# The opening's dummy products of a fused RWKV-6 and squared-ReLU kernel: 46 bf16 products become 12 fp32 products

## The chip, the cores and the metric

The kernel runs on one core of one Trainium2 chip. The metric is the device time of one execution in microseconds, the median of several runs. A profile is one execution recorded by the hardware profiler.

## The reference

Two stages. The first is a linear attention with a decaying state (4 batches, 8 heads, 768 positions, head size 48); the second is a two-layer network without gating on its output (3072 tokens, 384 to 2048 to 384), all in float32 at the interface.

```
for t in range(S):
    cur = einsum('bhd,bhe->bhde', u[None] * kt, vt)
    y[:, :, t] = einsum('bhd,bhde->bhe', rt, state + cur)
    state = wt[:, :, :, None] * state + einsum('bhd,bhe->bhde', kt, vt)
x = y, as (3072, 384)
h = x @ w_in;  g = max(h, 0)**2;  out = g @ w_out
```

## The kernel before

The 3072 tokens are cut into 12 steps of 256 positions (three for each batch), and a step into two chunks of 128. For each step the attention runs in the chunked form: logarithms of the decays (`ww_`, `lw_`), their running sums by products with triangular matrices (`cum_`, lines 324 to 328), exponentials (`exp_`, `ac_`), scaled copies of r and k (`rd_`), their transposes (`tr_` on TensorE with the copies `rkt_`, line 374, in the first steps; by DMA later), the score blocks (`p_`, line 420, masked in `pm_`), the state update (`su_`, `ts_`, `sn_`), the outputs (`y_`, `yc_`, `ysb_`) and their transposes for the second stage (`yt_`, `xt_`). The second stage is `m1_` (x times w_in, line 536, 48 products of 256 columns for a step in eight groups), a relu and a square (`rl_`, `sq_`, lines 545 to 555) and `m2_` (times w_out, line 561, 32 products of 384 columns), scaled out by `os_` and stored. All products of the two stages have bf16 operands.

The order of the work is written out by hand. `ORDER` is one string of words; the kernel goes through it word by word, and each engine issues its instructions in that order, with no reordering across words. A word is an operation with its arguments; what stands behind `=` is the engine (A ScalarE, V VectorE, G GpSimd), what stands behind `:` the PSUM banks. The loads (`ld.s.w`, `.k`, `.r`, `.v` of step s; `ld.g.i` and `ld.g.o` for the quarters of w_in and w_out) all go through SyncE's queue. w_in and w_out arrive as fp32 in four staging buffers and are cast to bf16 by the words `cast.i.g` and `cast.o.g` (line 200).

The change touches the word `warm_.n.i`: n products of the tile `warm`, which holds zeros, with itself, into a PSUM bank that is free at that point; nothing reads their result. `i` chooses the bank. There are eight such words, all among the first steps' work: with n = 11 and 8 ahead of and behind the first `cum_`, 3 and 5 around the transposes of step 0, 3 and 2 in step 0's output, 4 in step 1 and 10 ahead of the transposes of step 2. `warm` itself is cleared by the first instruction of `constants()` on VectorE (line 227), ahead of the other constants and of the zeros in `rdec_buf` and `kdec_buf`.

Of the kernel before, what the change touches and what calls it, by code (L numbers as in the profile page):

```python
# [8 lines left out]
FP32 = mybir.dt.float32  # L9
FP16 = mybir.dt.float16  # L10
BF16 = mybir.dt.bfloat16
# [3 lines left out]


ORDER = """
ld.0.w ld.0.k ld.0.r ld.0.u ld.1.w ww_.0=V lw_.0 warm_.11.5 cum_.0:0 kw_.0=G exp_.0 rd_.0.1 ld.0.v warm_.8.5
tr_.0.1:0 rkt_.0.1=A ld.1.k ld.1.r rw_.0=G ld.2.w ku_.0=G rd_.0.0 ld.1.v warm_.3.5 tr_.0.0:1 ww_.1=V
rkt_.0.0=A qp_.0=V ld.2.r v_.0=A warm_.5.5 p_.0.0:m p_.0.1:1 ac_.0 lw_.1 q_.0 su_.0:b ld.2.k cum_.1:0  # L20
ts_.0.0=A kw_.1=G pm_.0.0 pm_.0.1 vs_.0.0=A sn_.0.0 ld.1.i exp_.1 rw_.1=G vs_.0.1=A qs_.0=A rd_.1.1 ku_.1=G
warm_.3.2 yc_.0.1:1 ld.0.i ac_.1 ts_.0.1=V rd_.1.0 warm_.2.2 tr_.1.1:0 sn_.0.1 y_.0:1 rkt_.1.1=A vq_.0=V
tr_.1.0:1 ww_.2=G ld.2.i v_.1=A rkt_.1.0=V ysb_.0=V vs_.1.1=A warm_.4.2 p_.1.1:0 qp_.1=G su_.1:m ld.2.v
pm_.1.1 lw_.2 yt_.0:0 cum_.2:1 ld.3.i ts_.1.0=V rw_.2=G q_.1 exp_.2 kw_.2=G xt_.0=V vs_.1.0=A rd_.2.0 qs_.1=G
ac_.2 cast.i.1=A rd_.2.1 warm_.10.1 tr_.2.0:1 sn_.1.0 p_.1.0:0 ku_.2=G ts_.1.1=V yc_.1.1:1 tr_.2.1:0
cast.i.0=A pm_.1.0 ld.0.o m1_.0.3:0 ld.3.w rkt_.2.1=V m1_.0.2:1 vq_.1=G rkt_.2.0=V y_.1:1 rl_.0.3=A yc_.1.0:1
rl_.0.2=V p_.2.0:0 m1_.0.1:0 ld.1.o ysb_.1=V cast.i.2=G m1_.0.0:1 rl_.0.1=A pm_.2.0 yt_.1:0 ld.3.r rl_.0.0=A
m1_.0.5:0 v_.2=A xt_.1=V qp_.2=G sn_.1.1 m1_.0.4:1 rl_.0.5=A p_.2.1:1 su_.2:b sq_.0.0=A rl_.0.4=V ld.2.o
# [68 lines left out]
def kernel(  # L97
# [17 lines left out]
    C = 128  # L115
# [21 lines left out]
    consts = ctx.enter_context(tc.tile_pool(name="consts", bufs=1))  # L137
# [71 lines left out]

    warm = consts.tile([C, 512], BF16)
    tri_strict = consts.tile([C, C], BF16)
    tri_incl_neg = consts.tile([C, C], BF16)
    ident = consts.tile([C, C], BF16)
# [367 lines left out]
    def ld(n, x, h=None):  # L583
# [3 lines left out]
        ld=ld, cast=cast, ww_=ww_, lw_=lw_, v_=v_, vs_=vs_, rw_=rw_, kw_=kw_, ku_=ku_, qp_=qp_, q_=q_, qs_=qs_,  # L587
        vq_=vq_, cum_=cum_, al_=al_, exp_=exp_, ac_=ac_, rd_=rd_, tr_=tr_, rkt_=rkt_, dtr_=dtr_, p_=p_, pm_=pm_,
        su_=su_, ts_=ts_, sn_=sn_, y_=y_, yc_=yc_, ysb_=ysb_, yt_=yt_, xt_=xt_, dyt_=dyt_,
# [42 lines left out]
```

## Time and profile before

| | |
|---|---|
| time, median of 3 runs | 182.44 us (182.27 to 183.0) |
| span of the profiled execution, first to last instruction | 182.2 us |
| instructions | 5695 |
| TensorE busy | 171.8 us, 94% |
| VectorE, ScalarE, GpSimd busy | 130.0, 132.7, 122.7 us |
| dummy products (line 578) | 46, the first at 1.2 us, the last at 24.0 us |
| DMA, mean over the span | 197 GB/s |

The profile has no time of the execution beside its span; the median of the runs lies 0.24 us above the span. Times in the views count from the first instruction. PE is TensorE's products, PEld its weight loads, DVE VectorE, ACT ScalarE, POOL GpSimd, SPq SyncE's queue of loads and stores. A product's length is its latency; products overlap, so what one adds to the stream is read from the distance of two starts.

### The profile page before, as it was taken

The page shows a single profiled execution, that of the slowest core. Times are in us where ns is not written, and L with a number is a line of the kernel's source. Part 1 is how long each engine was busy: PE and PEld are TensorE (multiplying, and loading weights), DVE is VectorE, ACT ScalarE, POOL GpSimd, SP SyncE. Part 2 cuts the span into 40 slices and gives each one's busy share as a digit, 9 for nine tenths or more (in the row PEclk, how much of TensorE's full clock was granted, in tenths as well). Part 3 has the DMA queues.
Part 4 walks back from the last instruction along what each step waited for, and adds up shares of the span by engine and source line. Part 5 has one row for each costly group of instructions (what it writes and reads, how often), then busy time and mean ns, then how long its engine had stood idle before and what let it go on. Part 6 is the DMA issues. An engine that isn't in the chain of part 4 may idle for free.

```text
span 182.2 us, 5695 instructions
## 1 busy us (share of the span) xinstructions
PE 171.8 (94%) x2385; PEld 123.4 (68%) x2385; DVE 130.0 (71%) x195; ACT 132.7 (73%) x235; POOL 122.7 (67%) x140
## 2 busy tenths in 40 slices
PE   7986787999999999999899999999999999999992
PEld 2453556788686777777677777786877767777761
DVE  5488998787795998796677989885779675355120
ACT  4289665999779998869987997667979268552631
POOL 6539994999768999997949999699599413000000
PEclk9999999999999999999999999999999999999998
DMA  5999899999999989899999999997859520250023
GB/s 138 263 263 240 221 359 350 337 314 311 234 274 230 261 158 270 99 247 130 239 296 205 193 270 172 252 189 193 171 109 195 150 47 0 86 144 33 0 86 130
DMA packets 79208, 35.81 MB, mean 197 GB/s; under 512 B 72400, under 2 KB 77648, under 8 KB 79184
## 3 DMA queue, kind: packets, MB, share of 16 engines
q1 hardware_dynamic: 79184, 35.46, 85.9%
q8 instruction: 18, 0.29, 0.7%
q14 instruction: 6, 0.05, 0.1%
HBM read 25.36 MB, written 4.72 MB: 165 GB/s over the span
## 4 chain that ended last, share of the span: by engine, by line
PE 75%; SPq 10%; DMA 8%; ACT 4%; issue 1%; DVE 1%; ACTq 0%
PE bk L561 32%; PE m L536 32%; SPq L178 8%; DMA w_st<-in_moe_w_in_dram 5%; PE att L420 3%; DMA rT<-rdec_buf 2%; PE att L483 2%; PE att L493 2%; PE att L446 1%; ACT gt L545 1%; PE att L326 1%; ACT wi_sb L200 1%; PE bk L516 1%; SPq L188 1%; SPq L205 1%
## 5 line engine op out<-in xcount | busy, mean ns | idle before, releaser
L536 PE MATMUL m<-xT,wi_sb 128*128 128x256 bf16 x576 | 74.0, 273 | 1.3 <-ACT gt L545 1.2
L561 PE MATMUL bk<-wo_sb,gt 128*128 128x384 bf16 x384 | 71.9, 326 | 0.0
L536 PEld LDWEIGHTS <-wi_sb 128*128 128x128 bf16 x576 | 54.8, 98 | 13.0 <-issue 0.9
L561 PEld LDWEIGHTS <-gt 128*128 128x128 bf16 x384 | 36.9, 98 | 19.2
L545 ACT ACTIVATE gt<-m 128x512 f16<-128x512 f32 x56 | 33.0, 595 | 22.3 <-PE m L536 21.9
L553 ACT ACTIVATE gt<-gt 128x1024 bf16<-128x1024 f16 x42 | 43.3, 1051 | 1.4 <-DVE gt L547 1.1
L547 DVE TENSOR_SCALAR gt<-m 128x512 f16<-128x512 f32 x40 | 27.0, 686 | 9.6 <-PE m L536 9.3
L434 DVE TENSOR_TENSOR pmT<-att,mask 128x1024 bf16<-128x1024 f32 x20 | 23.9, 1218 | 4.5 <-PE att L420 4.5
L297 POOL TENSOR_TENSOR ku<-k_raw,u_bc 128x768 f32<-128x768 f32 x12 | 21.8, 1819 | 0.2 <-DMA u_bc<-in_u_dram 0.2
L302 POOL TENSOR_TENSOR ku<-ku,r_raw 128x768 f32<-128x768 f32 x11 | 20.7, 1881 | 0.2
L316 POOL TENSOR_TENSOR ku<-v_sh,qs 128x768 f32<-128x768 bf16 x11 | 16.3, 1479 | 4.9 <-ACT qs L277 4.8
L277 ACT CAST v_sh<-v_raw 64x384 bf16<-64x384 f32 x34 | 17.3, 508 | 0.4
L290 POOL TENSOR_TENSOR k_raw<-k_raw,w_raw 128x384 f32<-128x384 f32 x12 | 12.2, 1013 | 6.4 <-DMA k_raw<-in_k_dram 6.3
L286 POOL TENSOR_TENSOR r_raw<-r_raw,w_raw 128x384 f32<-128x384 f32 x12 | 12.0, 1000 | 6.4 <-DMA r_raw<-in_r_dram 6.4
L504 DVE TENSOR_TENSOR y_sb<-att,ku 128x768 bf16<-128x768 f32 x12 | 11.4, 953 | 5.5 <-issue 1.6
L461 POOL TENSOR_TENSOR S<-t_state,ac_buf 128x192 bf16<-128x192 f32 x20 | 10.2, 512 | 6.4 <-DVE t_state L456 3.4
L361 DVE TENSOR_TENSOR kdec_buf<-k_raw,att 128x768 bf16<-128x768 f32 x12 | 11.4, 949 | 3.4 <-ACT att L340 2.8
L358 DVE TENSOR_TENSOR rdec_buf<-r_raw,att 128x384 bf16<-128x384 f32 x24 | 12.1, 547 | 2.2 <-ACT att L340 1.1
L340 ACT ACTIVATE att<-att 128x768 f32<-128x768 f32 x12 | 9.6, 798 | 3.1 <-PE att L328 1.9
L568 ACT ACTIVATE o_sb<-bk 128x384 f32<-128x384 f32 x13 | 6.3, 485 | 7.4 <-PE bk L561 7.3
L307 DVE TENSOR_REDUCE q<-ku 128x16 f32<-128x768 f32 x12 | 11.3, 943 | 0.0
L578 PE MATMUL att<-warm 128*128 128x512 bf16 x27 | 9.1, 492 | 1.2 <-DVE half_ones L228 1.2
(80 smaller groups left out, 188.8 us busy)
## 6 DMA issues: line engine op xcount, KB each, us to landing
w_raw<-in_w_dram SPq DMA_DIRECT2D x12, 384.0 KB, 5.3
k_raw<-in_k_dram SPq DMA_DIRECT2D x12, 384.0 KB, 5.9
r_raw<-in_r_dram SPq DMA_DIRECT2D x12, 384.0 KB, 5.7
v_raw<-in_v_dram SPq DMA_DIRECT2D x12, 384.0 KB, 5.8
out_dram<-o_sb SPq DMA_DIRECT2D x24, 192.0 KB, 2.5
w_st<-in_moe_w_in_dram SPq DMA_DIRECT2D x4, 768.0 KB, 11.1
w_st<-in_moe_w_out_dram SPq DMA_DIRECT2D x4, 768.0 KB, 9.3
rT<-rdec_buf SPq DMA_TRANSPOSE x16, 4.1
```

Source lines behind the costliest of these rows:

```text
L178: nc.sync.dma_start(out=t[:, hs, at:at + 2, :].rearrange("p h j d -> p h (j d)"), in_=src[b, hs, i * T:(i + 1) * T, :].rearrange("h (p j) ...
L277: copy(out[j * Q:(j + 1) * Q, c], src[c * Q:(c + 1) * Q, :, j])
L290: tensor_mul("kw_", s, h)(raw["k", s][:, hs, 0, :], raw["k", s][:, hs, 1, :], raw["w", s][:, hs, 1, :])
L297: tensor_mul("ku_", s, h)(tiles["ku", s][:, hs], raw["k", s][:, hs, 1:3, :], u_bc[:, hs, None, :].to_broadcast([C, n, 2, D]))
L302: tensor_mul("qp_", s, h)(ku, ku, raw["r", s][:, heads(h), 0:2, :])
L316: tensor_mul("vq_", s)(vq[:], tiles["vs", s][:], tiles["qs", s][:, :, :, None].to_broadcast([C, 2, H, D]))
L434: nc.vector.tensor_mul(pmT, ps_p[:].rearrange("p e (x t) -> p (e x) t", t=C), mk.to_broadcast([C, 8, C]))
L536: nc.tensor.matmul(ps1[:, j, :], wi_sb[:, n // 4, kk, n % 4 * 128:(n % 4 + 1) * 128], tiles["xT", s][:, :, kk, :], start=(kk == 0), stop=( ...
L545: nc.scalar.activation(rl, m1, AF.Relu, scale=RS)
L547: nc.vector.tensor_scalar(out=rl, in0=m1, scalar1=RS, scalar2=0.0, op0=ALU.mult, op1=ALU.max)
L553: nc.scalar.activation(gt, rl, AF.Square)
L561: nc.tensor.matmul(m2, gt[:, n, c * C:(c + 1) * C], wo_sb[:, n, :], start=(n == 0), stop=(n == NT - 1))
```

## The change

The tile `warm` becomes fp32, and the eight counts are divided by about four: 11, 8, 3, 5, 3, 2, 4, 10 become 3, 2, 1, 1, 1, 1, 1, 2. The words keep their places in the order and their banks. The rest of the order and of the kernel is the same.

```diff
 ORDER = """
-ld.0.w ld.0.k ld.0.r ld.0.u ld.1.w ww_.0=V lw_.0 warm_.11.5 cum_.0:0 kw_.0=G exp_.0 rd_.0.1 ld.0.v warm_.8.5
-tr_.0.1:0 rkt_.0.1=A ld.1.k ld.1.r rw_.0=G ld.2.w ku_.0=G rd_.0.0 ld.1.v warm_.3.5 tr_.0.0:1 ww_.1=V
-rkt_.0.0=A qp_.0=V ld.2.r v_.0=A warm_.5.5 p_.0.0:m p_.0.1:1 ac_.0 lw_.1 q_.0 su_.0:b ld.2.k cum_.1:0
+ld.0.w ld.0.k ld.0.r ld.0.u ld.1.w ww_.0=V lw_.0 warm_.3.5 cum_.0:0 kw_.0=G exp_.0 rd_.0.1 ld.0.v warm_.2.5
+tr_.0.1:0 rkt_.0.1=A ld.1.k ld.1.r rw_.0=G ld.2.w ku_.0=G rd_.0.0 ld.1.v warm_.1.5 tr_.0.0:1 ww_.1=V
+rkt_.0.0=A qp_.0=V ld.2.r v_.0=A warm_.1.5 p_.0.0:m p_.0.1:1 ac_.0 lw_.1 q_.0 su_.0:b ld.2.k cum_.1:0
...
-warm_.3.2 yc_.0.1:1 ld.0.i ac_.1 ts_.0.1=V rd_.1.0 warm_.2.2 tr_.1.1:0 sn_.0.1 y_.0:1 rkt_.1.1=A vq_.0=V
-tr_.1.0:1 ww_.2=G ld.2.i v_.1=A rkt_.1.0=V ysb_.0=V vs_.1.1=A warm_.4.2 p_.1.1:0 qp_.1=G su_.1:m ld.2.v
+warm_.1.2 yc_.0.1:1 ld.0.i ac_.1 ts_.0.1=V rd_.1.0 warm_.1.2 tr_.1.1:0 sn_.0.1 y_.0:1 rkt_.1.1=A vq_.0=V
+tr_.1.0:1 ww_.2=G ld.2.i v_.1=A rkt_.1.0=V ysb_.0=V vs_.1.1=A warm_.1.2 p_.1.1:0 qp_.1=G su_.1:m ld.2.v
...
-ac_.2 cast.i.1=A rd_.2.1 warm_.10.1 tr_.2.0:1 sn_.1.0 p_.1.0:0 ku_.2=G ts_.1.1=V yc_.1.1:1 tr_.2.1:0
+ac_.2 cast.i.1=A rd_.2.1 warm_.2.1 tr_.2.0:1 sn_.1.0 p_.1.0:0 ku_.2=G ts_.1.1=V yc_.1.1:1 tr_.2.1:0
...
-    warm = consts.tile([C, 512], BF16)
+    warm = consts.tile([C, 512], FP32)
```

## The prediction

> **What bounds the kernel now.** I read the page first: the span, the busy engines, the clock and the chain that ended last.
>
> ```profile
> span 182.2 us, 5695 instructions
> ...
> PE 171.8 (94%) x2385; PEld 123.4 (68%) x2385; DVE 130.0 (71%) x195; ACT 132.7 (73%) x235; POOL 122.7 (67%) x140
> ...
> PEclk9999999999999999999999999999999999999998
> ...
> PE 75%; SPq 10%; DMA 8%; ACT 4%; issue 1%; DVE 1%; ACTq 0%
> ```
>
> TensorE carries three quarters of the chain. The other 18% of DMA and its queue need a place, because the change touches only the opening. So the second view was the chain in order of time, for its first 48 us. From 1.87 us on it is nothing but the load queue, and it ends like this:
>
> ```profile
> 17.59 1.33 SPq L188
> ...
> 18.96 9.57 DMA w_st<-in_moe_w_in_dram
> ...
> 28.55 1.47 ACT wi_sb L200
> 30.02 0.51 ACT gt L545
> ...
> 30.57 1.47 PE m L536 x12
> ```
>
> The load of a quarter of w_in lands at 18.96 + 9.57 = 28.53, ScalarE casts it, a relu queued behind that cast frees a bank of m1, and at 30.57 TensorE gets its next first-layer product. Nothing that TensorE did earlier is on this chain. After 30.57 the chain is TensorE nearly all the way. So the opening's products matter in three ways only: if they come so late that they are still running at 30.57, if they make the loads late, or if they change the clock at which the rest runs.
>
> The third view is TensorE's own row of time for the opening. The columns are start, length, engine, line, operation, tiles, count, and the idle time before it with what ended that.
>
> ```profile
> 1.19 4.87 PE L578 MATMUL att<-warm 128*128 128x512 bf16 x11 [1.19 <-DVE half_ones L228]
> 5.85 0.29 PE L324 MATMUL att<-half_ones,lw_buf 128*128 128x2 bf16 x4
> ...
> 6.60 2.14 PE L578 MATMUL att<-warm 128*128 128x512 bf16 x8
> 8.74 0.62 PE L374 MATMUL bk<-ident,kdec_buf 128*128 128x128 bf16 x8
> 9.20 0.81 PE L578 MATMUL att<-warm 128*128 128x512 bf16 x3
> 9.84 0.61 PE L374 MATMUL bk<-ident,rdec_buf 128*128 128x128 bf16 x8
> ...
> 15.25 0.31 PE L493 MATMUL att<-S,rT 64*64 64x48 bf16 x16 [0.88 <-DVE pmT L434]
> 15.50 0.61 PE L578 MATMUL m<-warm 128*128 128x512 bf16 x2
> 16.16 0.62 PE L374 MATMUL bk<-ident,kdec_buf 128*128 128x128 bf16 x8
> ...
> 17.81 0.23 PE L374 MATMUL bk<-ident,rdec_buf 128*128 128x128 bf16 x1 [0.62 <-DVE rdec_buf L358]
> ...
> 22.11 2.32 PE L578 MATMUL bk<-warm 128*128 128x512 bf16 x10
> 24.51 0.23 PE L374 MATMUL bk<-ident,rdec_buf 128*128 128x128 bf16 x1
> ...
> 28.94 0.40 PE L420 MATMUL att<-rT,kT 64*64 64x128 bf16 x16
> 30.57 1.47 PE L536 MATMUL m<-xT,wi_sb 128*128 128x256 bf16 x12 [1.23 <-ACT gt L545]
> ```
>
> TensorE stands idle for 1.23 us ahead of 30.57. That is the cover under which an opening that is late disappears.
>
> **What a dummy costs, and the clock.** The same line L578 in three stretches (1 to 5.5 us, 6.5 to 7.5, 9 to 11.4), and its weight loads over the span; the columns are count, then shortest, median and longest in ns.
>
> ```profile
> L578 PE MATMUL att<-warm x11: 607/634/634, 1.2 to 5.4; 128*128 128x512 bf16 x11
> ...
> L578 PE MATMUL att<-warm x4: 379/398/627, 6.6 to 7.5; 128*128 128x512 bf16 x4
> ...
> L578 PE MATMUL att<-warm x8: 379/379/379, 9.2 to 11.2; 128*128 128x512 bf16 x8
> ...
> L578 PEld LDWEIGHTS <-warm x46: 96/98/151, 1.2 to 23.8; 128*128 128x128 bf16 x46
> ```
>
> The page's clock line reads 9 from its first slice on, but one and the same product takes 634 ns until 5.4 us and 379 ns from 9.2 us, with the change between 6.6 and 7.5. So TensorE starts slow and comes up about 6 us after its first dummy. The starts give what one product adds to the stream: (5.85 − 1.19) / 11 = 0.424 us slow, (9.84 − 9.20) / 3 = 0.213 us fast. The weight load (98 ns) fits under the product before it.
>
> **The change, part by part.**
>
> *Counts.* 46 dummies become 12, in the same eight places: 11, 8, 3, 5, 3, 2, 4, 10 become 3, 2, 1, 1, 1, 1, 1, 2. As built, each fp32 product is one instruction, without the separate weight load that each bf16 one had. DVE, ScalarE, GpSimd and the load queue keep their order.
>
> *Price of an fp32 product.* The trace has none. The lower bound is a bf16 product of that shape, 0.424 slow or 0.213 fast. For the upper one, I split each wide number into two narrow halves: four partial products, each with a weight load that nothing hides, 4 × (0.424 + 0.098) = 2.09 slow and 4 × (0.213 + 0.098) = 1.24 fast. I take four hidden passes, 1.70 slow and 0.85 fast, because in this kernel's stream of 512 columns the weight load of every dummy is hidden. The Trainium skill, "FP8 and Floating Point Precision", TensorE Precision Notes, also gives four passes for true fp32; no run here shows it yet. Passes by place are then 12, 8, 4, 4, 4, 4, 4, 8 against 11, 8, 3, 5, 3, 2, 4, 10: 48 against 46.
>
> *The clearing of the dummy tile* doubles in bytes. The VectorE and ScalarE rows that this and the next steps need:
>
> ```profile
> 0.86 0.27 DVE L227 MEMSET warm<- 128x256 uint32 x1 [0.86 <-PEq L616]
> ...
> 1.55 0.48 DVE L232 MEMSET rdec_buf<- 128x512 uint32 x1 [0.17 <-issue]
> ...
> 4.57 0.56 DVE L264 TENSOR_TENSOR ww<-w_raw 128x384 f32<-128x384 f32 x1 [0.91 <-DMA w_raw<-in_w_dram]
> 7.73 0.95 DVE L361 TENSOR_TENSOR kdec_buf<-k_raw,att 128x768 bf16<-128x768 f32 x1 [2.60 <-ACT att L340]
> 8.60 1.01 DVE L358 TENSOR_TENSOR rdec_buf<-r_raw,att 128x384 bf16<-128x384 f32 x2
> 10.25 0.77 DVE L264 TENSOR_TENSOR ww<-w_raw 128x384 f32<-128x384 f32 x1 [0.63 <-DMA w_raw<-in_w_dram]
> ...
> 32.41 0.56 DVE L521 COPY xT<-bk 128x768 bf16<-128x768 bf16 x1 [0.99 <-PE bk L516]
> ```
>
> ```profile
> 5.22 0.52 ACT L268 ACTIVATE lw_buf<-ww 128x384 bf16<-128x384 f32 x1 [2.17 <-DVE ww L264]
> ...
> 25.24 1.47 ACT L200 CAST wi_sb<-w_st 128x1536 bf16<-128x1536 f32 x1
> 28.55 1.47 ACT L200 CAST wi_sb<-w_st 128x1536 bf16<-128x1536 f32 x1 [1.84 <-DMA w_st<-in_moe_w_in_dram]
> ```
>
> The clearing of 128x512 words took 0.48 in rdec_buf's row, so warm's goes from 0.27 to 0.48, +0.21. VectorE's later clearings move by 0.21 under the 0.91 us for which it waits for w_raw; the first dummy moves from 1.19 to 1.40.
>
> *First block (11 to 12 passes).* 1.40 + 12 × 0.424 = 6.49, against 5.85: the first cum_ starts 0.64 late. Its input, lw_buf, is there at 5.22 + 0.52 = 5.74, so the dummies do hold it back. At the ends of the price: with bare bf16 products it starts on time or 0.1 early, with exposed weight loads at 1.40 + 3 × 2.09 = 7.67, 1.82 late.
>
> *Behind it.* exp_ on ScalarE and rd_ on VectorE go 0.64 late. VectorE's two rd_ (7.73 to 9.61) end at 10.25, exactly where it waited 0.63 for w_raw anyway, so its queue is back on time there. Two fp32 products (1.70) behind the cum_ end (6.49 + 0.75 of cum_ + 1.70 = 8.94) before the late kdec_buf is ready (7.73 + 0.95 + 0.64 = 9.32), so they add nothing. The third block grows from 3 to 4 passes between two transposes: 0.64 + 0.21 = 0.85 late at 9.84. ScalarE's copies of kT and rT and the lw_, ac_ and exp_ of step 1 are queued behind those transposes and hand some 0.6 of it on.
>
> *Blocks 5 and 6* (3 to 4, 2 to 4 passes, +0.21 and +0.43) stand around a wait of 0.88 for pmT at 15.25 and ahead of one of 0.62 for rdec_buf at 17.81; both lie in that idle time. *Block 8* loses two passes (−0.43) but the transpose behind it at 24.51 is followed by rdec_buf's second half, not by the dummies' end; I count nothing.
>
> *What arrives at the dense part.* At most 0.85 us late, and nothing more is added behind. TensorE's last work ahead of the wait ends at 28.94 + 0.40 = 29.34, or 30.19 late by 0.85, ahead of 30.57. ScalarE's first cast ends at 25.24 + 1.47 = 26.71, or 27.56, ahead of the landing at 28.53 (1.84 idle). VectorE has 0.99 idle at 32.41. All three covers are larger than the delay. What is not covered: the load queue waits for that first cast before it starts its next load:
>
> ```profile
> 26.74 1.27 SPq L194 DMA_DIRECT2D w_st<-in_moe_w_out_dram  x1
> ```
>
> That load and those queued behind it slip by up to 0.85. They feed w_out and the third step, used some 10 us later. I take 0.1 of it as felt: a guess between 0 and 0.85.
>
> *Sum.* +0.64 + 0.21 − 0.85 covered + 0.1 = +0.1 on a span of 182.2. The median of the three runs is 182.44, 0.24 above the span, so the forecast is 182.5. At the dear end of the price the opening arrives 1.8 to 2.0 late, past TensorE's cover of 1.23 by 0.6 to 0.8: 183.2. At the cheap end it stays at 182.4, provided the clock still comes up.
>
> **The rivals.** A measurement can tell about 0.5% (0.9 us) from no change.
>
> *The clock does not come up (slower).* If an fp32 pass counts for less than a bf16 one in what opens the clock, TensorE stays slow through the opening. That decides as soon as the 6.6 to 7.5 us rise is missing. For the size, TensorE's busy time from there to the first dense wait:
>
> ```profile
> 7.10:30.50 23.40, 18.27 (x337) 11.32 (x336) 20.92 (x30) 16.38 (x29) 17.45 (x19) 1.00 1.08 280
> ```
>
> Of 23.40 us it is busy 18.27 and idle 5.13. Slow, the 36 dummy passes behind the first block add 36 × 0.211 = 7.6, and the kernel's own products there, some 18.3 − 34 × 0.213 = 11, add perhaps half of themselves, 5 (a good part of a short product's length is latency). 12.6 − 5.13 idle − 1.23 cover = +6, 188.5. A clock that comes up halfway costs half or less, 183.5 to 185.5. For it: the rise came in a stretch that was nearly all dummies, and nothing in the trace shows what fp32 does there. Against it: four passes keep the array as busy as the four products they replace. The Trainium skill, "TensorE: Matmul & The Clock Gate", Part 1, has the clock at half until some 3.4 us of sustained activity, and Part 4 names transposes alone as not counting as busy in the same way; by that this rival would not come about, and the trace agrees on the halves (0.424 and 0.213) while the rise took some 6 us. I give 0.20.
>
> *The passes are dearer than 0.85 (slower).* Exposed weight loads, or four-byte operands that stream more slowly: with its 1.23 of cover, TensorE loses 0.9 us from a delay of about 2.1 us on; at six slow passes a product the first block ends at 1.40 + 18 × 0.424 = 9.03, 3.2 late, and the kernel loses 2: 184.4. Against it: every weight load of the dummies hides now. The Trainium skill, "TensorE: Matmul & The Clock Gate", Weight-path perf modes, says that fast weight load is off for fp32; that speaks for this rival, and no row here shows such a load. I give 0.09.
>
> *Faster.* It needs w_in's load to land earlier or a shorter dense part; no step of the change reaches either. The instruction stream is shorter by some 80 instructions, which could leave the loads of the opening freer; if the 9.57 us landing shrank by a tenth, 181.5. I give 0.09.
>
> *The change does not do what it says:* excluded by the program as built, where the 46 pairs are gone and 12 fp32 products stand there.
>
> **How the numbers follow.** The forecast has 0.62, its own range 182.2 to 183.3 from the lowest run of before, the dear end of the price and the slipping loads. Same is 0.62. Slower is 0.29: the clock 0.20, dear passes 0.09. Faster is 0.09. The range must leave out at most 0.2: 181.8 below leaves out most of the faster case (0.06); 185.5 above takes in the dear passes and a clock that comes up halfway, and leaves out about 0.13 of a clock that is lost.
>
> **What would show it.** Right: the first cum_ near 6.5 instead of 5.85; each fp32 product worth 0.85 at full clock; TensorE's idle time before 30.57 shrunk from 1.23 to 0.4 or so with the start itself unmoved; the cast at 28.55 still released by the DMA. Wrong: short products still at their slow lengths after 8 us; the m1 product at 30.57 released by something other than the relu behind that cast; a stream of fp32 products whose starts are more than 0.9 us apart at full clock.

## The result and the profile after

The changed kernel takes 183.34 us (median of 17 runs, 182.05 to 184.38), the kernel before on the same chip 182.27 us (17 runs, 181.58 to 183.0). The ratio is 1.0051, with a 95% interval from 1.0028 to 1.0074: slower by 0.9 us by the ratio, at the very edge of what the prediction counted as no change. The forecast was 182.5 us, with a range of 181.8 to 185.5. The ratios here and below leave out runs of more than 1.5% above the fastest of their kernel (two each of e3 and e10, one of the kernel before), so a ratio can be smaller than that of the two medians.

The profiled execution of the changed kernel took 183.43 us. Its page, the lines that answer to those of before:

```profile
span 181.7 us, 5651 instructions
...
PE 172.5 (95%) x2363; PEld 123.3 (68%) x2363; DVE 129.6 (71%) x195; ACT 132.3 (73%) x235; POOL 123.0 (68%) x140
...
PEclk9999999999999999999999999999999999999998
...
PE 72%; DMA 10%; POOL 6%; SPq 3%; ACT 3%; DVE 2%; issue 1%; ACTq 0%; POOLq 0%; DVEq 0%
```

The chain no longer starts with 10% of load queue (SPq). There are 44 instructions fewer, not some 80. TensorE's row of time for the opening shows the twelve products as 24 records:

```profile
1.45 5.35 PE L578 MATMUL att<-warm 128*128 128x512 f32 x6 [1.45 <-DVE half_ones L228]
6.64 0.24 PE L324 MATMUL att<-half_ones,lw_buf 128*128 128x2 bf16 x4
...
7.07 1.88 PE L578 MATMUL att<-warm 128*128 128x512 f32 x4
...
10.53 0.61 PE L374 MATMUL bk<-ident,rdec_buf 128*128 128x128 bf16 x8
...
16.50 0.62 PE L374 MATMUL bk<-ident,kdec_buf 128*128 128x128 bf16 x8
...
21.87 1.88 PE L578 MATMUL bk<-warm 128*128 128x512 f32 x4
24.27 0.23 PE L374 MATMUL bk<-ident,rdec_buf 128*128 128x128 bf16 x1 [0.53 <-DVE rdec_buf L358]
...
29.03 1.48 PE L536 MATMUL m<-xT,wi_sb 128*128 128x256 bf16 x12
```

The delay of the opening is there at first, and then shrinks: against before the first `cum_` is 0.79 us late (6.64 against 5.85), the first transposes of rdec_buf 0.69 (10.53 against 9.84), those of kdec_buf 0.34 (16.50 against 16.16), and at 24.27 the kernel is 0.24 early. The m1 product that stood behind 1.23 us of idle time at 30.57 now starts at 29.03 and waits for nothing. So this execution enters the dense part 1.5 us earlier than the profiled one of before, and yet the kernel is slower. The profile alone does not say where it loses: that is what the experiments are for.

One thing has to be put right before two traces are compared. In every run whose span is known (17 runs of after, and those of the experiments and of the kernel before beside them) the time is 1.73 to 1.85 us longer than the span. The profiled execution of before, with its span of 182.2 us, so took about 184.0 us (an estimate: 182.2 + 1.8), 1.0 more than the slowest of the three times shown with it. It was not a typical one.

### The profile page after: what moved, and what is told of

Its sections match the earlier page's. It is cut to its first block, busy times and chain, and to the rows that moved or that the text cites. A ratio compares the mean times of both kernels' runs of the same rounds, so it can differ in the third digit from the quotient of the medians.

```text
span 181.7 us, 5651 instructions
## 1 busy us (share of the span) xinstructions
PE 172.5 (95%) x2363; PEld 123.3 (68%) x2363; DVE 129.6 (71%) x195; ACT 132.3 (73%) x235; POOL 123.0 (68%) x140
## 4 chain that ended last, share of the span: by engine, by line
PE 72%; DMA 10%; POOL 6%; SPq 3%; ACT 3%; DVE 2%; issue 1%; ACTq 0%; POOLq 0%; DVEq 0%
PE m L536 30%; PE bk L561 29%; DMA k_raw<-in_k_dram 4%; PE att L420 3%; PE att L483 3%; DMA kT<-kdec_buf 3%; DMA xT<-y_sb 2%; PE att L493 2%; SPq L178 2%; DMA rT<-rdec_buf 2%; PE att L446 2%; POOL ku L302 1%; POOL k_raw L290 1%; POOL r_raw L286 1%; DVE kdec_buf L361 1%
## 5 line engine op out<-in xcount | busy, mean ns | idle before, releaser
L578 PE MATMUL att<-warm 128*128 128x512 f32 x14 | 9.4, 803 | 1.4 <-DVE half_ones L228 1.4
```

## Experiments

Each time is a median of twelve runs (ten of e7, six of e6), beside the kernel before on the same chip, as a ratio with its 95% interval. e1 to e4 shared one chip, e5 to e8 a second, e9 to e11 a third; e12 was timed last, by itself, on the second. The theories named in the expectations: A, the late opening costs time in itself; B, the blocks that became longer (5 and 6) do; C, the clock; and, from e9 on, I, the places where TensorE's instructions are fetched.

**e1: the kernel before, once more.** No edit.

> The kernel before, unchanged, profiled once more. If the profile of before that the prediction rests on was an execution with a late load of w_in (its span of 182.2 us lies near the changed kernel's 181.7 us although the medians are 182.27 and 183.34 us), this one shows a span of about 180.5 us, a time some 1.8 us above its span, and the m1 product that stood at 30.57 us starting near 28.5 to 29.3 us without a wait of 1.23 us ahead of it. If that profile was typical, the product stands at 30.5 again and the span is 182. Ratio 1.000 within 0.002 either way.

Measured: 182.89 us, ratio 0.9985 [0.9966, 1.0004]. Its profile is of the fastest of its twelve runs, 182.35 us with a span of 180.6. TensorE and ScalarE at the same place:

```profile
28.57 0.40 PE L420 MATMUL att<-rT,kT 64*64 64x128 bf16 x16
29.29 1.47 PE L536 MATMUL m<-xT,wi_sb 128*128 128x256 bf16 x12 [0.32 <-ACT gt L545]
```

```profile
27.27 1.47 ACT L200 CAST wi_sb<-w_st 128x1536 bf16<-128x1536 f32 x1 [1.08 <-DMA w_st<-in_moe_w_in_dram]
```

The cast still waits for the load, but 1.08 us instead of 1.84, and TensorE 0.32 instead of 1.23. The cover on which the prediction leaned is here a quarter of what it read. It changes from execution to execution: the same wait is 1.1 us in e2's profile, and e4's has none. Against this execution the changed kernel is 0.26 us earlier at that product (29.03 against 29.29).

**e2 and e3: the two halves of the change.** e2 makes only the first block fp32, e3 only the other seven.

```diff
 e2, e3: warm is fp32; a bf16 block reads it as bf16
+        z = warm[:] if not warmed else warm[:].bitcast(BF16)[:, 0:512]      # e2
+        z = warm[:].bitcast(BF16)[:, 0:512] if not warmed else warm[:]      # e3
 counts, before:  11, 8, 3, 5, 3, 2, 4, 10
+e2:               3, 8, 3, 5, 3, 2, 4, 10
+e3:              11, 2, 1, 1, 1, 1, 1, 2   (and warm is cleared in two halves, the second behind the others)
```

> Only the first block is fp32 (3 products, ahead of the first cum_), all other dummies are bf16 as before; the tile is cleared whole, as in the change. Theory A (the opening arrives late: the first cum_ starts 0.6 to 0.8 us later and in most executions no late load covers that) expects most of the loss here: ratio 1.003 to 1.006. Theory B (the fp32 products behind the first block cost it, through their weight loads at the edges of the blocks) expects 1.000 to 1.001. Theory C (fp32 counts less for the clock, so that in some executions it comes up later) expects 1.003 to 1.006 with runs in two groups, because the rise falls into or just behind this block.

> The first block stays bf16 (11 products, half of the tile cleared ahead of them as before, the other half behind the other constants), the seven later blocks are fp32. Theory A expects 1.000 to 1.002, theory B 1.004 to 1.006, theory C 1.000 to 1.003.

Measured: e2 182.83 us, 0.9984 [0.9966, 1.0003]; e3 184.04 us, 1.0035 [1.0006, 1.0064]. The longer first block and the longer clearing cost nothing (in e2's profile the first `cum_` starts at 6.11 us, 0.26 late); the loss is with the later blocks, although e3's first block is not longer. Theory A falls.

**e4: the time of the change without its type.** bf16 throughout, with as many passes in each block as the fp32 version.

```diff
-counts: 11, 8, 3, 5, 3, 2, 4, 10
+counts: 12, 8, 4, 4, 4, 4, 4, 8
```

> bf16 dummies in the number of the fp32 passes: 12, 8, 4, 4, 4, 4, 4, 8, the tile cleared as before. Theory A expects half of the loss: the first cum_ starts 0.43 us later by one product, without the 0.25 us of the longer clearing: 1.001 to 1.004. Theories B and C, for which it is fp32 itself, expect 1.000 to 1.001.

Measured: 182.65 us, 0.998 [0.9955, 1.0005]. The blocks' lengths are not it either, which leaves nothing of theory B but the type of the products, or whatever goes with it.

**e5 and e6: after and e3 again, on another chip.** No edit to either.

> The changed kernel, unchanged, on the chip of this group and profiled once more. If its loss is real and not that chip's, the ratio is 1.003 to 1.007 again. If the loss came from the load of w_in landing at other times by chance, it is 1.000 within 0.002.

> The first block bf16, the seven later ones fp32, as in the run of that name before. Its times there spread over 3.8 us. If the later blocks carry the loss, 1.003 to 1.006 and a wide spread again; by chance, 1.000 within 0.002 and a spread of 1.5 us, as the kernel before has.

Measured: e5 184.47 us, 1.0066 [1.004, 1.0092]; e6 184.6 us, 1.0074 [1.0051, 1.0098]. The loss is real, and the seven later blocks alone are enough for all of it.

**e7 and e8: a part of the later blocks.** Blocks 2 to 4 alone in fp32, or blocks 5 to 8 alone; `warm` is cleared in two halves as in e3.

```diff
+        z = warm[:] if len(warmed) in (1, 2, 3) else warm[:].bitcast(BF16)[:, 0:512]       # e7
+        z = warm[:] if len(warmed) in (4, 5, 6, 7) else warm[:].bitcast(BF16)[:, 0:512]    # e8
-counts: 11, 8, 3, 5, 3, 2, 4, 10
+e7:     11, 2, 1, 1, 3, 2, 4, 10
+e8:     11, 8, 3, 5, 1, 1, 1, 2
```

> Only the second, third and fourth block are fp32 (2, 1, 1 products), between the first cum_ and the first score blocks. Theory C (the clock comes up a good 3 us later in those executions in which the moment for it falls into or behind these blocks, because fp32 passes count less) expects the loss here: 1.003 to 1.006 with a wide spread. Theory B (fp32 passes come in fours, so that the fifth and sixth block last 0.2 and 0.4 us longer and hold back the transposes behind them) expects 1.000 to 1.001.

> Only the last four blocks are fp32 (1, 1, 1, 2 products), from the second cum_ on. Theory B expects the loss here: the transposes at 15.8 us 0.5 to 0.65 us later and 0.3 us of it at the dense part, 1.001 to 1.003. Theory C expects 1.000, because the clock is up by then in all profiles. A third, that the clock falls back for a while in the stretch between 13 and 25 us because fp32 passes count less, expects a granted clock below 0.995 in some runs and those runs slower.

Measured: e7 184.04 us, 1.0059 [1.0038, 1.008]; e8 183.84 us, 1.0027 [1.0001, 1.0053]. Neither group is innocent, though e8's loss is barely clear of the noise. Theory B falls with e7, where blocks 5 and 6 are as before. Theory C falls as well: the mean granted clock of after, e3, e5, e6, e7 and e8 was 0.996 or more in every run.

**Where TensorE waits.** With the opening cleared, the view of waits for TensorE from 28 us to 178 us; the columns are what waits, for what, us in total, times, longest. First e1, then after, then e5 (the same kernel as after):

```profile
PE m L536 <- ACT gt L545: 0.3, 1, 0.3
PE att L420 <- DMA rT<-rdec_buf: 0.3, 1, 0.3
```

```profile
PE att L420 <- DMA rT<-rdec_buf: 0.6, 1, 0.6
PE m L536 <- DMA xT<-y_sb: 0.4, 1, 0.4
```

```profile
PE att L420 <- DMA rT<-rdec_buf: 1.2, 1, 1.2
PE m L536 <- DMA xT<-y_sb: 0.7, 1, 0.7
PE m L536 <- ACT gt L545: 0.2, 1, 0.2
```

TensorE waits for transposes by DMA, some 45 to 113 us after the last dummy (68 and 137 us in after, 86 and 137 in e5); the wait for xT is in no profile of before. The view of DMA around this transposition (its window from issue to landing, and the 1.5 us or so ahead of it) has one more line than expected. First e1, ahead of the issue at 131.41 and then from it on:

```profile
q8 instruction: 1, 0.02, 8.4%
```

```profile
xT<-y_sb SPq DMA_TRANSPOSE x1, 2.8
```

and then after, ahead of its issue at 132.04 (where no instruction packet stands) and from it on:

```profile
rT<-rdec_buf SPq DMA_TRANSPOSE x1, 2.9
```

```profile
q8 instruction: 1, 0.02, 1.3%
...
xT<-y_sb SPq DMA_TRANSPOSE x1, 4.4
```

The number at the end of an issue's line is the time to landing. A packet of TensorE's instructions is fetched just before this transposition in e1, and it lands in 2.8 us; in after the fetch falls inside, and it lands in 4.4 us. The page of both kernels has 18 such packets, 0.29 MB, so 16 KB each; in the trace of e1 the steps between them are some 250 TensorE instructions on average. The Trainium skill, "Runtime: NRT & Kernel Launch", Instruction fetch mechanics, says that instructions are streamed in 16 KiB blocks of 256 by a DMA queue of the engine's own, and calls this mostly hidden. The trace agrees on the size; none of TensorE's waits in these views is for a fetch, but the transposition beside one is longer.

That makes a theory. Four bf16 dummies are eight instructions, an fp32 product is four (two weight loads, two products). So after executes 44 instructions fewer in the opening, and every later fetch comes at another place in the work. **Theory I:** not the type of the dummies but their number of instructions makes the loss.

**e9: the later blocks in fp32, the number of instructions as before.** e3 with a first block of 28 narrow bf16 products, which last as long as 11 wide ones.

```diff
 e3, but
-first block: 11 bf16 products of 512 columns
+first block: 28 bf16 products of 201 columns
```

> The seven later blocks are fp32 as in e3 and e6; the first block is 28 bf16 products of 201 columns instead of 11 of 512 (an estimate of the same time, 28 x 0.168 = 4.7 us against 11 x 0.427), so that TensorE executes as many instructions as in the kernel before and its instruction fetches come at the same instructions again. Theory I (the loss comes from where the instruction fetches fall, and they moved because fp32 dummies are fewer instructions): ratio to before 0.998 to 1.002, fetches of the middle part near 67.8 and 131 us again. Rival (the loss comes from the later blocks being fp32, through something else): 1.004 to 1.007 as in e3 and e6.

**e11: after, with the number of instructions restored in its last block.**

```diff
 after, but
-last block: 2 fp32 products of 512 columns
+last block: 26 bf16 products of 128 columns
```

> The changed kernel, but its last block (two fp32 products, 1.71 us) is 26 bf16 products of 128 columns (an estimate of 26 x 0.056 = 1.5 us), so that from about 24 us on TensorE has executed as many instructions as in the kernel before; the fetches before that come as in the changed kernel, the later ones as in the kernel before. Theory I, with the loss in the late fetches: ratio 0.999 to 1.002. Theory I with the loss in the early fetches, or the rival (fp32 itself): 1.004 to 1.007.

Measured: e9 183.04 us, 1.0014 [0.9996, 1.0031]; e11 182.87 us, 1.0002 [0.9974, 1.0031]. Both keep the later fp32 blocks (e11 all but the last), and no loss is left that the measurement can tell, although three of the twelve runs of e11 had a mean clock of 0.987 or 0.991: e6, with the same seven blocks as e9, had 1.0074 [1.0051, 1.0098]. In both the fetch is ahead of the transposition again and the landing is short; e9's window ahead of the issue at 132.16, then from it on:

```profile
q8 instruction: 1, 0.02, 3.9%
```

```profile
xT<-y_sb SPq DMA_TRANSPOSE x1, 2.8
```

**e10 and e12: the number of instructions changed, the later blocks bf16.** The opposite test. e10 has 40 instructions fewer, e12 has 212 more, which with a fetch every 250 should put the late fetches where some 38 fewer put them.

```diff
-counts: 11, 8, 3, 5, 3, 2, 4, 10
+e10:     3 (fp32), then bf16: 4, 3, 2, 3, 2, 4, 2
+e12:     28 of 201 columns, then 28, 11, 18, 11, 7, 15, 34 of 128 columns, all bf16
```

> No fp32 product in the seven later blocks: they are bf16 with 4, 3, 2, 3, 2, 4 and 2 products, and only the first block is fp32 with three products (as e2, which lost nothing). TensorE executes 40 instructions fewer than before, about as many fewer as after (44) and e3 (34). Theory I: ratio 1.003 to 1.007, with waits of TensorE for transposes near 68, 86 or 137 us. Rival (fp32 in the later blocks itself): at most 1.001. With fewer dummies the granted clock can lose a window in the opening; that would show as a mean clock of about 0.99 and does not count for either.

> All dummies are bf16 and their blocks keep their times (28 products of 201 columns, then 28, 11, 18, 11, 7, 15 and 34 products of 128 columns, an estimate of 0.062 us each from the 26 products in 1.61 us of e11), but they are 106 products more, which is 212 TensorE instructions. The fetches come every 250 instructions (mean of the kernel before: 17 steps from instruction 280 to 4535), so 212 more put the late fetches where 38 fewer would, about as in the kernel after (44 fewer), with no fp32 and no lower clock. Theory I in its strong form (the places of the late fetches suffice): 1.003 to 1.007. fp32 itself, or theory I needing something else besides: 0.998 to 1.002.

Measured: e10 183.78 us, 1.0035 [1.001, 1.0061]; e12 183.25 us, 1.0039 [1.0004, 1.0074]. Both as theory I has it, but neither time settles it. In e10, with its fewer dummies, the clock fell for a while, as the granted clock (the third figure from the end) of its windows around the start of the dense part shows:

```profile
20.00:24.00 4.00, 2.04 (x62) 1.31 (x61) 4.00 (x7) 2.91 (x6) 3.74 (x6) 1.00 0.96 304
24.00:28.00 4.00, 3.07 (x53) 2.35 (x54) 3.64 (x7) 1.69 (x3) 3.88 (x5) 0.82 1.00 343
28.00:30.00 2.00, 2.00 (x21) 1.50 (x19) 0.85 (x3) 1.82 (x2) 0.23 (x2) 0.51 1.09 369
```

Nine of its twelve runs had a mean clock of 0.991 or less, and two of e12's twelve had 0.991, at 184.39 and 184.89 us; without these two e12's median is 183.0, only 0.1% above before. The traces are clearer than the times. In both the fetch falls inside the transposition, with no fp32 product anywhere behind the first block; e10 from 132.32 on, then e12 from 130.93 on:

```profile
q8 instruction: 1, 0.02, 1.3%
...
xT<-y_sb SPq DMA_TRANSPOSE x1, 4.4
```

```profile
q8 instruction: 1, 0.02, 1.8%
...
xT<-y_sb SPq DMA_TRANSPOSE x1, 4.4
```

All fourteen profiles on one scale: the instructions executed against before, where the fetch fell, how long the transposition took to land, and the time from the 385th to the 433rd product of line 536 (one step of m1, worked out from their starts).

| kernels | instructions | fetch | landing, us | 48 products of m1, us |
|---|---|---|---|---|
| before, e1, e2, e4, e9, e11, e7, e8 | −18 to +4 | 0.46 to 0.71 us ahead of the issue | 2.8 to 2.9 | 10.43 to 10.44 |
| e3, e6, e10, after, e5 | −34 to −44 | 2.0 to 2.5 us behind it | 4.4 to 4.8 | 10.91 to 11.32 |
| e12 | +212 | 1.3 us behind it | 4.4 | 10.96 |

There is no exception and no overlap. A fetch inside this one transposition costs it 1.5 to 2.0 us, and the kernel 0.5 to 0.9 us at this place. That is about half of what separates the profiled executions from e1's: 0.55 of 1.1 us in after (10.99 against 10.44, in spans of 181.7 and 180.6 us) and 0.88 of 1.8 us in e5 (11.32, in a span of 182.4).

About as much again arises between 60 and 88 us, where TensorE waits for rT; behind 36 us and outside these two stretches the steps of m1 agree within 0.2 us in all fourteen profiles. The 96 products of m1 from the 145th to the 241st take 26.27 us in e1, 26.86 in after and 27.25 in e5. But this stretch changes by up to 1.8 us in one and the same program (25.83 in e3, 27.64 in e6), so one profile of each kernel does not tell how much of a median's loss belongs here.

Two executions of one program also show the fetch moved while the number of instructions is kept. The view of DMA from the issue of the second transposition of rT near 82 us, for some 2.4 us, first in e5 and then in after, where no instruction packet stands yet:

```profile
q8 instruction: 1, 0.02, 3.0%
...
rT<-rdec_buf SPq DMA_TRANSPOSE x1, 4.5
```

```profile
rT<-rdec_buf SPq DMA_TRANSPOSE x1, 2.9
```

The fetch starts 2.32 us behind the issue in e5 and 2.42 us behind it in after. In e5 TensorE waits 1.2 us for this landing, in after not at all, and the 48 products of m1 around it take 13.84 and 12.72 us. In all fourteen profiles this transposition lands in 2.8 to 2.9 us where the fetch starts 2.35 us or more behind its issue (five), and in 3.6 to 4.5 us where it starts earlier (nine).

## Why the prediction was right or wrong

The time lies in the forecast's range, but not by the sum that led there. The sum's +0.1 us stood for loads that slip behind a late opening, and no run shows such a loss; the 0.9 us came by a term that stood at nothing. That they stayed near the limit of what counts as no change is luck.

**The price of an fp32 product: right.** Two records of 591 ns whose starts at full clock are (1.88 − 0.59) / 3 = 0.43 apart, so 0.86 a product against 0.85 taken; slow, (6.64 − 1.45) / 12 = 0.43 a pass against 0.424. The trace now agrees with the four passes of the Trainium skill, "FP8 and Floating Point Precision", TensorE Precision Notes, though it shows them as two products, each behind a weight load. The line's rows from 6.9 to 10 us:

```profile
L578 PEld LDWEIGHTS att<-warm x6: 188/190/192, 6.9 to 9.7; 128*128 128x128 f32 x6
L578 PE MATMUL att<-warm x5: 591/592/649, 7.1 to 9.6; 128*128 128x512 f32 x5
```

The load takes 190 ns where the bf16 one took 98, and hides behind the 0.43 of the product before it. So the rival of dear passes falls.

**The clearing: right.**

```profile
0.91 0.48 DVE L227 MEMSET warm<- 128x512 f32 x1 [0.91 <-PEq L616]
```

0.48 as taken from rdec_buf's row.

**The late first block: harmless, as said, and right in size by luck.** 6.64 against 6.49. The prediction took the whole block at the slow pace. In e5, an execution of the same program, the pace doubles inside the block:

```profile
5.93 0.25 PE L324 MATMUL att<-half_ones,lw_buf 128*128 128x2 bf16 x4
```

There the first `cum_` is 0.08 us late, and yet this run, with 184.15 us, is slower than the profiled one of after. e2 shows too that the longer block costs nothing.

**The clock: the rival falls.** The records of 7.07 us already start 0.43 us apart, which is 0.215 a pass, and in after, e3 and e5 to e9 the mean clock was never below 0.996. fp32 passes keep the clock up like the bf16 ones that they replace.

**The cover: mis-sized.** "TensorE stands idle for 1.23 us ahead of 30.57" is true of that one execution; the wait is 0.32 in e1, 1.1 in e2, and nothing in e4 and after. The step behind it, "The median of the three runs is 182.44, 0.24 above the span", was wrong by 1.5 us: the time is 1.73 to 1.85 above the span, so that profile was of an untypical execution. It did no harm, because the opening's delay had melted away before the dense part: by the pauses, and in this execution by a VectorE product (line 316) that took 1.10 us instead of 1.68 for a reason that the trace does not show. The score products behind it start at 20.23 us, 0.24 before those of the kernel before, and so ahead of the shorter last block (21.87 us), to which the prediction had given nothing. The forecast that the start at 30.57 stays unmoved fell with the cover.

**What was left out: the loss.** The sum had two ways to lose time behind the opening, lateness and the load queue ("I take 0.1 of it as felt"). The loss came by neither. It is in "The instruction stream is shorter by some 80 instructions, which could leave the loads of the opening freer": the count was 44, the effect was seen, and it was put among the gains. In the opening it looks like a gain at first. The issue of the k_raw load of step 2, in the queue of loads, after and then before:

```profile
14.38 1.45 SPq L178 DMA_DIRECT2D k_raw<-in_k_dram  x1
```

```profile
14.62 2.92 SPq L178 DMA_DIRECT2D k_raw<-in_k_dram  x1
```

In before an instruction packet is fetched during this issue, in after none. But in after the packet falls into the loads of w_in behind it: their first three issues take 4.04 us instead of 2.40 and end at 19.91 us, against 19.99 in before. In e5, the same program as after, the fetch is back inside the issue of k_raw, which takes 2.85 us. And what moves one fetch moves all behind it too, to the end of the kernel, and one fell on a transposition that TensorE waits for. The term for it should have been open to both signs.

**What stays open.** How much of the loss in the medians comes from the stretch between 60 and 88 us. e7 and e8 are slower by 0.6% and 0.3% with their fetch ahead of the xT transposition; their 96 products there take 27.34 and 26.84 us (26.27 in e1), with waits for rT of 1.1 us near 88 us and 0.6 us near 68 us, each in the one execution profiled. Near 69 us the issue of kT lasts 3.36 to 4.16 us in the nine profiles in which a fetch starts inside it, and 2.22 to 3.29 in the other five. The nine are all those of kernels with a loss, e7 and e8 among them, and e2, which has it long (4.16) and lost nothing in its median; but where the issue is short, a load issued just before it is longer.

That the fetch itself lengthens the transposition, rather than something else that goes with the number of instructions, rests on the fourteen cases without exception, on e9, e11, e10 and e12, which moved it in both directions, and on the transposition near 82 us, where it moved in one program. Which fetches do harm is open: near 140 us one that starts 2.5 us behind the issue of kT leaves the landing at 3.0 to 3.1 us (e1, e9, e11), and one 2.8 us behind it goes with 4.8 (before, e4). And e5 and e6, beside which e9 and e11 show no loss, ran on another chip than these; the traces do not depend on that.

No version beat before by more than the measurement can tell: e4 with 0.998 [0.9955, 1.0005] is the lowest.

## What to carry to other kernels

Read time and span together before arguing from a profile: if one profiled execution is 1.5 us above the median, so are the idle times that serve as cover; and for a difference of half a per cent one profile of each kernel is too few. When a change alters the number of instructions on an engine, even at a place where it costs nothing, compare the instruction packets in the DMA view of both traces all the way to the end, above all inside transposes that TensorE waits for. A padded variant with the same count (narrow products of the same total time) tells in one run whether a small loss is the change's own or that of its places.

## What the hardware showed that was not expected

- One instruction packet of 16 KB that starts 1.3 to 2.5 us behind the issue of a DMA transposition of 2.8 us goes with a landing after 4.4 to 4.8 us (xT near 132 us). At other transpositions a fetch late in the window left the landing as it was.
- An fp32 product of 512 columns is recorded as two weight loads (190 ns) and two products (591 ns), 0.86 us in all at full clock and 1.73 at half.
- 128-column bf16 products follow one another at (23.30 − 21.91) / 25 = 0.056 us (e11), so narrow products give the number of instructions a knob of its own. The estimate of 0.062 us behind e12 was too high, and its blocks of 128 columns came out a tenth shorter than meant.
- The clock came down to 0.51 for 28 to 30 us in e10, where from 20 to 24 us TensorE had been busy for 2.04 of 4.00 us; with 3.42 us in after and 3.33 in e5 it stayed at 1.00.
